# Loading q by pairs of tokens in the attention front of a RetNet and PReLU-MLP kernel, with a new instruction order

## The chip, the cores and the metric

The kernel runs on one core of a Trainium2 chip. The metric is device time in microseconds (us) of one execution; the times are medians of repeated runs.

## The reference

The attention is a retention layer without softmax; its output, seen as 4608 tokens of 512 features, goes through a two-layer MLP with a PReLU.

```python
# q, k, v: (8, 8, 576, 64) = batch, head, token, feature, float32
scores = matmul(q, k^T) / 8
gamma = 1 - 2 ** (-5 - head)
ret = scores * where(rel >= 0, gamma ** rel, 0)      # rel = row - column
attn = matmul(ret, v)
x = attn.transpose(0, 2, 1, 3).reshape(4608, 512)
h = x @ w_in                                          # w_in: 512 x 2048
g = maximum(h, 0) + alpha * minimum(h, 0)             # alpha: one per column of h
out = g @ w_out                                       # w_out: 2048 x 512
```

All inputs are float32; the two weights and alpha reach the kernel as 64-bit words, and it makes float32 of the weights itself.

## The kernel before

**Attention.** The 576 tokens of a head are nine chunks of 64. Within a chunk the scores are computed and masked; what earlier chunks contribute comes through a running state per head (64 x 64). The decay gamma is split into factors that depend on the token alone, so q, k and v only have to be scaled by tables (`tp`, made from `pf`, `dif` and `th` on DVE at the start).

**The front: parts.** The first two batches are done in six parts: parts 0, 1, 2 are chunks 0 to 3, 4 to 7 and 8 of batch 0, and parts 3, 4, 5 the same of batch 1. Parts 0, 1, 3 and 4 are the large ones. For a large part, `load_part` loads k, q and v as two tiles each (256 KB, 128 tokens in the partitions, eight heads of 64 features beside each other), so that the rows which the DMA moves have 64 floats (256 B). `part_scale` multiplies q and v by a table on POOL, in place. `part_transposes` turns k and q on PE, four 128x128 transposes for each tile, into a PSUM bank, and ACT copies them into SBUF. `part_scores` multiplies turned k and q by chunk on PE and masks on DVE into a room of its own (`at`). `part_states` and `part_values` make the states and the outputs, which ACT copies into x. `last_part` does the small parts. All later batches go pair by pair of heads through `joint`.

**The MLP.** Eight cells of the MLP run in the front with plain float32 matmuls (`unit_plain`, `second_plain`); `convert` makes their weights out of 64-bit words on ACT, DVE and POOL. The other cells use a split of x, g and the weights into pieces of lower precision (`split_roll`, `unit_roll`, `unit_two`, `second`), with matmuls of 128x128 by 512 columns.

**Dummy matmuls.** `fill` and `burn` put matmuls of a zero tile (`warm`) on PE at the start of the front; their results are not read.

**What sets the order.** Nothing is scheduled while the kernel is built. Each step is recorded by `do(engine, cost, function, reads, writes)` and gets a number; the list `ORDER` says in which order the steps are issued, which fixes the sequence on each engine, and the string `BANKS` says which PSUM bank each step gets. All loads and stores but one are issued by SP's queue. In the first `LIMITED` places of the order, a load also waits until at most `IN_FLIGHT` bytes (`IN_FRONT` in the first `FRONT` places) are under way:

```python
    LIMITED, IN_FLIGHT = 486, 5 << 18
    FRONT, IN_FRONT = 130, 4 << 18
```

POOL and DVE steps that are marked `lock=True` follow each other through a dependency in that order, across the two engines.

Of the kernel before, what the change touches and what calls it, by code (L numbers as in the profile page):

```python
# [10 lines left out]
FP32 = mybir.dt.float32  # L11
# [6 lines left out]
ALU = mybir.AluOpType  # L18
# [3 lines left out]
def kernel(  # L22
# [110 lines left out]
    for o, x, y in ((slice(0, 2), slice(0, 2), slice(3, 5)), (0, 0, 1), (0, 0, 2), (1, 0, 5)):  # L133
# [5 lines left out]
                                   in1=pf[:, 6], op0=ALU.mult, op1=ALU.mult)  # L139
    nc.vector.tensor_scalar(th[:, 2], dif[:, 6], 1.0, None, ALU.add)  # L140
# [8 lines left out]
    for i in range(2):  # L149
# [6 lines left out]
        "200535545661702405070423172047436234654317545707176141645461704500066171106600717116602607"  # L156
        "060167247052344635472107161067706117062653241061707601706104253461761006176107255234700761"
# [62 lines left out]
    RATE, RATE_256, RATE_128 = 265e3, 205e3, 115e3  # L220
# [17 lines left out]
    LIMITED, IN_FLIGHT = 486, 5 << 18  # L238
# [96 lines left out]

    def load_part(x, which=None):
        j0, j1 = PARTS[x % 3]
        for i, m in which or [(i, m) for i in range(3) for m in range((j1 - j0 + 1) // 2)]:
            s0 = (j0 + 2 * m) * C
            rows = min(P, j1 * C - s0)  # L340
            dma(lambda i=i, m=m, rows=rows: part(x, i)[0:rows, m],
                lambda i=i, s0=s0, rows=rows: (k, q, v)[i][x // 3, :, s0:s0 + rows].rearrange(
                    "h p d -> p h d"), rows * DM * 4, (), [key_p(x, i, m)], rate=RATE_256)

    def part_scale(x, i):
        j0, j1 = PARTS[x % 3]
        rows = min(P, (j1 - j0) * C)
        for m in range((j1 - j0 + 1) // 2):
            def f(m=m):
                t = part(x, i)[0:rows, m]  # L350
                return nc.gpsimd.tensor_tensor(
                    out=t, in0=t, in1=tp[0:rows, i - 1, m, :, None].to_broadcast([rows, H, D]),
                    op=ALU.mult)
            do("POOL", 1.05, f, (), [key_p(x, i, m)], lock=True)
# [8 lines left out]
    def part_transposes(x, i, bank):  # L363
# [6 lines left out]
        for m in range(2):  # L370
            pt = Gen(next(bank))

            def f(m=m, pt=pt):
                for c in range(NPAIR):
                    nc.tensor.transpose(pt.get()[:, c * P:(c + 1) * P],
                                        part(x, i)[:, m, 2 * c:2 * c + 2].rearrange(
                                            "p h d -> p (h d)"), ident)
            do("PE", 0.52 if x else 0.65, f, [key_p(x, i, m)], [(pt, 0)], size=8)

            def g(m=m, pt=pt):  # L380
                nc.scalar.copy(at()[:, :, m * P:(m + 1) * P],
# [3 lines left out]
    def part_scores(x, bank):  # L385
        a = Gen((gs[1], ats)[x // 3]) if x % 3 == 0 else room[x + 1, 2]

        def at():
            return words_of(a)[:, 0:1024].rearrange("p (h n) -> p h n", h=2)
        tat[x] = a, at  # L390
        (kt, kT), (qt, qT) = tT[x, 0], tT[x, 1]
        ps = [Gen(next(bank)) for _ in range(2)]
        for m in range(2):
            def f(m=m):
# [7 lines left out]
            do("PE", 0.58, f, [(kt, "t", m), (qt, "t", m)], [(ps[0], m), (ps[1], m)], kind="small",  # L402
               size=64)
        for h2 in range(2):
# [5 lines left out]
            do("DVE", 0.69, g, [(ps[h2], 0), (ps[h2], 1)], [(a, "m", h2)])  # L410
# [45 lines left out]
    def part_values(x, bank):  # L456
# [28 lines left out]
        for m in range(2):  # L485
# [16 lines left out]
            do("PE", 0.29 * len(js), g, [(qt, "t", m)] + [  # L502
# [1052 lines left out]
    for i, (va, vb) in enumerate(two):  # L1555
# [30 lines left out]
        "68-70 67 3 71 1-2 0 4-5 53 24 66 12 25 86 9 13-14 33 16 10 15 22 7 17 80 23 19 8 85 32 47 18 21 20 "  # L1586
        "27 48-50 84 6 115 83 51 26 64 55 52 28-29 56-57 87 81 118 58 119 88 30 59 62 82 63 40 114 116 65 60 "
        "154 112 34 31 54 117 110 113 11 72 111 36-37 139 61 136 138 140 38 142 35 153 141 137 171 41 43-44 "
        "89 39 42 168 143 94 166 144 95 103 73 145 90 45 146 46 155 147 181 156-157 209 182 75 170 183 76-77 "
        "102 158 74 159 91 93 160 92 212 161 184 162-163 204 78 121-122 97 176 185 129 96 98 177 99 104 100 "  # L1590
        "173 205 124 106 164 105 120 208 169 337 101 188-189 130 107-109 213 123 132 172 196 125-126 148 210 "
        "149 127 167 133 150 246 197 131 211 229 206-207 152 134-135 330 230 151 190 192-194 217 216 218 178 "
        "180 186 247 179 257 219 244 198 128 270 220 250 221 331 199 245 187 332 175 191 200 271 201-202 174 "
        "222 454 223 234-235 203 224-227 333 195 284-285 231 236 293 259 336 272 456 237 451 238-239 232-233 "
        "292 228 274 258 453 455 248 275 273 260-261 252 262 251 445 276 243 253 452 249 214 254 242 255 240 "
        "263 241 277 286 349 447 266 288 268 289-290 267 269 215 372 256 294 296-298 287 291 303 302 306 342 "
        "374 304 295 305 282 466 307 281 338 334 299 278 436 279 264 350 265 280 446 340 343 315 352-353 339 "
        "335 345 354 351 448 439 316 344 346 358 365 317 553 384 347 355 348 320 366 321 318-319 373 308 475 "
        "322 375 341 433 309 437 385 301 399 435 442 552 300 377 398 310-312 323-324 328 313 378 434 325 443 "
        "283 379 383 327 329 314 367 369 368 440 438 356 450 382 457 376 460 381 326 397 441 380 462 404 461 "  # L1600
        "79 415 414 360 467 413 361 405-410 402 458 411 400 412 417 419 359 362 416 363 423 422 421 165 364 "
        "403 401 444 392 463 393 386 459 387 468 357 465 481 555 482 420 424 449 388 418 394 426 464 396 425 "
        "472 490 370 473 395 522 488 519 523 483 520 526 489 495 529 487 507 469 496 389 497-498 390 499 524 "
        "501 505 427 506 478 504 517 500 503 539 493 485 568 371 502 428 492 484 521 530 527 476 528 534-535 "
        "540 532 541 516 508 533 430 391 542 491 536 543 537 544 494 545 470 538 582 486 514 474 480 581 509 "
        "583 477 510 512 511 513 515 431 471 618 595 584 531 588 570 590 596 546 597-599 569 586 563 548 585 "
        "594 547 593 571 549 564 607 587 479 601 604 600 561 589 616 562 565 620 572 566-567 573-575 606 554 "
        "592 634 603 619 605 636 602 577 591 432 635 617 614 551 608 576 615 610 550 637 578 621 638-639 "
        "622-623 640 651 609 612 655 624 652 429 648 641 653 611 613 658-661 654 662 674 579 643 665-668 656 "
        "697 647 669 663 670 695 671 696 664 688 672-673 690 675 689 580 677 687 657 649 642 644 698 645 650 "  # L1610
        "699-701 691-694 686 721 684 676 702 704 720 679 678 722 685 730 518 723 703 758 705 734-735 680-681 "
        "646 726 683 729 682 711 761 727 762 733 717 706 759 728 724 746 763 707-708 716 736 712 781 731 737 "
        "744 754 772 760 738-740 783 713-714 756 718 709 774-775 784 743 732 741 755 742 782 556 773 745 747 "
        "785-786 525 751 719 779 776 787 710 752-753 777 725 780 748 778 840 749-750 715 794-796 793 807 841 "
        "805 802 789 788 790 798 797 842 803 808-809 800 817 791 804 833 799 810 834 811-812 814 831 813 816 "
        "820 832 843 806 819 815 852 818 801 835 854 828-829 853 830 792 855-856 918 915 557 838 821 827 857 "
        "916 824 836 858 822 837 877 859 823 919 880 826 878 861 920 879 860 885 887 881 891 886 892-893 825 "
        "894 839 895 889 901 864 897 873 896 869 900 899 888 862 868 870-871 898 917 903 883 902 875 863 930 "
        "932 884 931 882 874 890 923 933 558-559 912 921 934 865-866 924 904 935 914 922 910 928 913 936 905 "
        "907 925 943 911 872 944 906 908 945-946 926-927 999 955 952 929 967 957 953 966 958-959 956 909 937 "  # L1620
        "954 876 948 960-962 939 942 969 949 951 991 1002 938 940 947 979 950 963 965 1004 968 998 1000 1003 "
        "1005-1007 992 964 867 757 971 989-990 993 1008 994 997 978 560 970 976 995 941 1028 625 1027 974 "
        "1029 1038 1001 977 1009 973 1010 975 1011 1050 1037 1041 1030 1068 1012 996 1065 1013 1042 1069 1014 "
        "1066 1015 1018 1067 1019 1051 1016 1071 1036 1035 972 1043-1044 1072 1020 1070 1073 1053 1034 1045 "
        "1047 1024 1046 1089 1033 1074-1075 1040 1049 1091 1048 1090 1063 1076 1052 1021 1079 1077 1092 1032 "
        "1055 1093 1039 1094 1060 1054 1064 1061 1095 1023 1017 1025-1026 1062 1031 1078 1059 1102 1056 1103 "
        "1111 1105 1104 1112 1141 1097 1110 1116 1106 1096 1098 1115 1099 1107 1100 1058 1113 1125 1148 1139 "
        "1057 1127 1117-1120 1122 1109 1121 1142 1114 1140 1126 1154 1150 1128 1152 1108 1153 1155 1143-1145 "
# [179 lines left out]
```

## Time and profile before

| | |
|---|---|
| median of 3 runs | 915.4 us (915.34 to 915.81) |
| the profiled execution's own time | 915.47 us |
| its span, first to last instruction | 913.4 us |
| PE busy | 906.3 us (99%) |
| DVE, ACT, POOL busy | 549.6, 500.7, 520.3 us |
| DMA share, 0 to 30 us and 30 to 112 us | 0.99 and 0.92 |
| DMA share, 112 to 913 us | 0.47 |

The profile is one execution. Busy times are of instructions, and an engine's idle time matters only where the engine that ends last waits for it. Times below that begin with a start are microseconds from the span's start. PE is TensorE's matmuls, PEld its weight loads, DVE VectorE, ACT ScalarE, POOL GpSimd, SP the engine whose queue issues the DMAs.

### The profile page before, as it was taken

What the parts mean: (1) busy time and instruction counts of PE and PEld (TensorE: products, weight loads), DVE (VectorE), ACT (ScalarE), POOL (GpSimd) and SP (SyncE); (2) the same over time, 40 slices, a digit from 0 to 9 for tenths busy, and PEclk for the clock granted to TensorE, in tenths of its full rate; (3) what the DMA queues carried; (4) which work ended last, traced back from release to release, by engine and by line L of the source; (5) the groups of instructions that cost most, each with busy time, mean ns of one, the idle gap of its engine ahead of it and who ended that gap; (6) DMA issues with size and microseconds to landing.
All of it is one profiled execution on the core that took longest, in us unless ns stands there. A gap on an engine that the chain in (4) does not pass through costs nothing. (4 is left out here: it accounts for less than half of the span.)

```text
span 913.4 us, 19163 instructions
## 1 busy us (share of the span) xinstructions
PE 906.3 (99%) x7331; PEld 739.6 (81%) x7331; DVE 549.6 (60%) x1004; ACT 500.7 (55%) x1011; POOL 520.3 (57%) x461
## 2 busy tenths in 40 slices
PE   9999999999999999999999999999999999999998
PEld 8767788887788888888888888888888888888886
DVE  5797767757768776576756776434444534444243
ACT  4575665556555665666746565636363636364441
POOL 4587665556556665756542335666655657574624
PEclk9999999999999999999999999999999999999999
DMA  9999778788898888775243332212122222211112
GB/s 204 245 232 185 172 173 184 166 204 186 185 200 192 205 208 189 177 182 167 70 141 130 99 115 82 70 58 81 57 93 64 91 82 76 93 47 47 46 47 70
DMA packets 235948, 121.34 MB, mean 133 GB/s; under 512 B 203456, under 2 KB 203728, under 8 KB 235856
## 3 DMA queue, kind: packets, MB, share of 16 engines
q1 hardware_dynamic: 235712, 119.98, 52.3%
q8 instruction: 58, 0.95, 0.5%
q14 instruction: 34, 0.28, 0.1%
q10 hardware_dynamic: 144, 0.13, 0.0%
HBM read 74.19 MB, written 32.51 MB: 117 GB/s over the span
## 5 line engine op out<-in xcount | busy, mean ns | idle before, releaser
L1223 PE MATMUL pso<-w,g 128*128 128x512 f32 x1344 | 330.3, 392 | 0.0
L1223 PEld LDWEIGHTS pso<-w,g 128*128 128x128 f32 x1344 | 249.9, 188 | 54.3 <-POOL g L1150 1.6
L1147 POOL TENSOR_TENSOR g<-ga_all,g 128x512 fp32r<-128x512 f32 x76 | 98.2, 1295 | 131.5 <-ACT g L1143 101.8
L1150 POOL TENSOR_TENSOR g<-g 128x512 fp32r<-128x512 f32 x114 | 147.3, 1295 | 19.4 <-DVE su L949 5.7
L1071 PE MATMUL psa<-lx_x,w 128*128 128x512 f32 (+1 forms) x288 | 70.3, 377 | 0.2 <-DVE at L824 0.2
L1071 PE MATMUL psh<-lx_x,w 128*128 128x512 f32 (+1 forms) x272 | 68.2, 384 | 0.1
L1143 ACT ACTIVATE g<-ga_all 128x512 fp32r<-128x512 f32 x76 | 47.8, 631 | 36.6 <-PE pso L1223 17.5
L1139 POOL TENSOR_TENSOR g<-g 128x512 fp32r<-128x512 f32 x22 | 28.5, 1297 | 61.8 <-DVE g L1136 34.4
L1071 PEld LDWEIGHTS psa<-lx_x,w 128*128 128x128 f32 x288 | 51.4, 188 | 12.1 <-issue 1.3
L1071 PEld LDWEIGHTS psh<-lx_x,w 128*128 128x128 f32 x272 | 49.6, 188 | 11.2 <-issue 0.6
L1223 PE MATMUL pso<-lx_x,g 128*128 128x512 f32 x216 | 53.5, 390 | 0.1
L1147 POOL TENSOR_TENSOR g<-vn,g 128x512 fp32r<-128x512 f32 x25 | 32.4, 1297 | 37.2 <-ACT g L1143 34.5
L1145 ACT ACTIVATE g<-ga_all 128x512 fp32r<-128x512 f32 x76 | 47.2, 624 | 5.8 <-PE pso L1223 4.0
L1046 POOL TENSOR_TENSOR lx_x<-lx_x 128x512 fp32r<-128x512 f32 x28 | 35.9, 1293 | 23.1 <-DVE lx_x L1043 18.9
L1223 PEld LDWEIGHTS pso<-lx_x,g 128*128 128x128 f32 x216 | 40.4, 188 | 9.0 <-DVE o L1246 0.6
L1241 DVE TENSOR_TENSOR op<-pso,op 128x512 f32<-128x512 f32 x35 | 24.0, 686 | 31.2 <-PE pso L1223 31.2
L1071 PE MATMUL pso<-lx_x,w 128*128 128x512 f32 (+1 forms) x160 | 37.8, 370 | 0.0
L1105 PE MATMUL psh<-w,w 128*128 128x512 f32 x144 | 34.6, 389 | 0.0
L1105 PE MATMUL psa<-w,w 128*128 128x512 f32 x144 | 34.6, 389 | 0.0
L716 POOL TENSOR_TENSOR qx<-qx,tabx 128x576 f32<-128x576 f32 x24 | 27.6, 1149 | 9.6 <-DMA qx<-in_q_dram 5.9
L1071 PEld LDWEIGHTS pso<-lx_x,w 128*128 128x128 f32 x160 | 28.0, 188 | 5.7 <-ACT o L1245 0.6
L1147 POOL TENSOR_TENSOR g<-x,g 128x512 fp32r<-128x512 f32 x13 | 16.9, 1298 | 26.2 <-ACT g L1143 24.7
(408 smaller groups left out, 1968.2 us busy)
## 6 DMA issues: line engine op xcount, KB each, us to landing
xk<-x SPq DMA_DIRECT2D x18, 512.0 KB, 3.7
ok<-o SPq DMA_DIRECT2D x36, 256.0 KB, 2.7
op<-ok SPq DMA_DIRECT2D x18, 512.0 KB, 4.0
out_dram<-o SPq DMA_DIRECT2D x35, 256.0 KB, 2.3
x<-xk SPq DMA_DIRECT2D x16, 512.0 KB, 5.5
kx<-in_k_dram SPq DMA_DIRECT2D x96, 72.0 KB, 3.3
qx<-in_q_dram SPq DMA_DIRECT2D x96, 72.0 KB, 3.3
kn<-in_k_dram SPq DMA_DIRECT2D x48, 144.0 KB, 3.6
```

The lines of the kernel that those rows point to most:

```text
L716: return nc.gpsimd.tensor_tensor(out=qh, in0=qh, in1=tabx[:, None, c, :, None].to_broadcast([P, NJ, 2, 32]), op=ALU.mult)
L1046: do("POOL", 1.29, lambda h=h, l=l, d=d: nc.gpsimd.tensor_tensor(out=piece(d()), in0=h(), in1=l(), op=ALU.subtract), [(g, 0, n), (g, 1, n) ...
L1071: nc.tensor.matmul(out_of(p), w[:, c0:c0 + P], xp(l, cc), start=(l != 1 and cc == 0), stop=(l > 0 and cc == NCC - 1))
L1105: nc.tensor.matmul(p.get(), w[:, c0:c0 + P], piece(words_of(g)[:, o:o + DM]), start=(l != 1 and cc == 0), stop=(l > 0 and cc == NCC - 1))
L1139: do("POOL", 1.29, lambda: nc.gpsimd.tensor_tensor(out=piece(to.get()[:, 2]), in0=to.get()[:, 0], in1=to.get()[:, 1], op=ALU.subtract), [( ...
L1143: do("ACT", 0.64, lambda: nc.scalar.mul(piece(to.get()[:, 2]), whole(), BELOW), both, [(to, 2)])
L1145: do("ACT", 0.64, lambda: nc.scalar.mul(piece(to.get()[:, 0]), whole(), BELOW * 2.0 ** -12), both, [(to, 0)])
L1147: do("POOL", 1.29, lambda: nc.gpsimd.tensor_tensor(out=piece(to.get()[:, 1]), in0=whole(), in1=to.get()[:, 2], op=ALU.subtract), both + [( ...
L1150: do("POOL", 1.29, lambda: nc.gpsimd.tensor_tensor(out=piece(to.get()[:, 2]), in0=to.get()[:, 0], in1=to.get()[:, 1], op=ALU.subtract), [( ...
L1223: nc.tensor.matmul(a[2 * m + b].get(), piece(g.get()[:, l, f, m * P:(m + 1) * P]), w_piece(u, 2 + f, l), start=(cell["first"] and f == 0 a ...
L1241: do("DVE", 0.69, lambda: nc.vector.tensor_tensor(out=t(), in0=p1.get(), in1=t(), op=ALU.subtract), [(p1, 0)], [tk])
```

## The change

q of the four large parts is loaded so that a partition holds two neighbouring tokens of a head: 128 floats (512 B) in a row, for four heads at a time, and each such 256 KB is loaded by two DMAs of 128 KB, one for the even heads and one for the odd. POOL scales q by a new table `tq` (two columns for each head, one for each of the two tokens), no longer in place: it writes into the room that takes the masked scores later, with the heads in the order in which they are transposed. The transposes read that room; ACT's copy of their result puts the two tokens of a pair back beside each other (every second word). A transposed half now holds all 256 tokens of four heads, instead of 128 tokens of eight, so that scores and values name both halves. `ORDER` and `BANKS` are new for the first part of the program, and `LIMITED` goes from 486 to 500.

```diff
+    tq = const.tile([P, 2, 2 * NPAIR], FP32, name="tq")
+    tq_of = [tq.rearrange("p h (c e) -> p h c e", e=2)[:, :, :, e] for e in range(2)]
+    def by_pairs(t):
+        return t.rearrange("p (c h) -> p h c", h=2)
+    nc.vector.scalar_tensor_tensor(out=tq_of[0], in0=by_pairs(tp[:, 0, 0]), scalar=1.0 / QSCALE,
+                                   in1=by_pairs(tp[:, 0, 0]), op0=ALU.mult, op1=ALU.mult)
+    nc.vector.scalar_tensor_tensor(out=tq_of[1], in0=by_pairs(dif[:, 0]), scalar=1.0,
+                                   in1=tq_of[0], op0=ALU.add, op1=ALU.mult)
...
-    LIMITED, IN_FLIGHT = 486, 5 << 18
+    LIMITED, IN_FLIGHT = 500, 5 << 18
...
+    def twos(x, i):
+        return i == 1 and x % 3 < 2
+    def part_q(x, m):
+        return spot_p(x, 1)[:, m * DM:(m + 1) * DM]
+    def turned_q(x, m):
+        return tat[x][1]().rearrange("p h n -> p (h n)")[:, m * DM:(m + 1) * DM]
     def load_part(x, which=None):
...
+            if twos(x, i):
+                for h2 in range(2):
+                    dma(lambda m=m, h2=h2: part_q(x, m).rearrange(
+                            "p (h c f) -> p h c f", h=2, f=P)[:, h2],
+                        lambda m=m, h2=h2: q[
+                            x // 3, 4 * m + h2:4 * m + 4:2, j0 * C:j1 * C].rearrange(
+                                "c (p e) d -> p c (e d)", e=2), P * DM * 2, (),
+                        [key_p(x, i, m) + (h2,)], rate=RATE_512)
+                continue
...
     def part_scale(x, i):
...
+        if twos(x, i):
+            a = Gen((gs[1], ats)[x // 3]) if x % 3 == 0 else room[x + 1, 2]
...
+                    return nc.gpsimd.tensor_tensor(
+                        out=turned_q(x, m).rearrange("p (n h d) -> p h n d", h=2, d=D),
+                        in0=part_q(x, m).rearrange("p (h n d) -> p h n d", h=2, d=D),
+                        in1=tq[:, :, 4 * m:4 * m + 4, None].to_broadcast([P, 2, 4, D]), op=ALU.mult)
+                do("POOL", 1.05, f, [key_p(x, i, m) + (h2,) for h2 in range(2)], [(a, "r", m)], lock=True)
+            return
...
     def part_transposes(x, i, bank):
...
-            do("PE", 0.52 if x else 0.65, f, [key_p(x, i, m)], [(pt, 0)], size=8)
+            do("PE", 0.52 if x else 0.65, f,
+               [(tat[x][0], "r", m) if twos(x, i) else key_p(x, i, m)], [(pt, 0)], size=8)
...
+                if twos(x, i):
+                    nc.scalar.copy(
+                        at()[:, 2 * m:2 * m + 2].rearrange("p c (t e) -> p c e t", e=2),
+                        pt.get().rearrange("p (c e t) -> p c e t", c=2, e=2))
+                    return
...
     def part_scores(x, bank):
...
-            do("PE", 0.58, f, [(kt, "t", m), (qt, "t", m)], [(ps[0], m), (ps[1], m)], kind="small",
-               size=64)
+            do("PE", 0.58, f, [(kt, "t", m), (qt, "t", 0), (qt, "t", 1)], [(ps[0], m), (ps[1], m)],
+               kind="small", size=64)
...
-            do("DVE", 0.69, g, [(ps[h2], 0), (ps[h2], 1)], [(a, "m", h2)])
+            do("DVE", 0.69, g, [(ps[h2], 0), (ps[h2], 1)], [(a, "m", h2), (a, "r", h2)])
...
-            do("PE", 0.29 * len(js), g, [(qt, "t", m)] + [
+            do("PE", 0.29 * len(js), g, [(qt, "t", 0), (qt, "t", 1)] + [
```

What the new `ORDER` does, as the built program shows it: SP's first loads were k, q, q, k, v, v of part 0 (256 KB each) and are now q, q (128 KB each), v, q, q, k, k, v. A q load of part 3 now stands ahead of the small part's k, and the k of part 4 stands later. On PE the steps up to the 112th are in another order, from the 113th on in the same one; on the other engines the steps after that stretch stand in the same order too. SP issues eight loads more, DVE runs two instructions more, PE, ACT and POOL have as many as before.

## The prediction

> **What bounds the kernel now.** I read the busy shares first, then PE's waits, then PE's and SP's timelines of the first 30 us, because the built programs differ only there (below).
>
> ```profile
> span 913.4 us, 19163 instructions
> ...
> PE 906.3 (99%) x7331; PEld 739.6 (81%) x7331; DVE 549.6 (60%) x1004; ACT 500.7 (55%) x1011; POOL 520.3 (57%) x461
> ...
> q8 instruction: 58, 0.95, 0.5%
> ```
>
> PE has something to do in all but 7 us. The last line is the instruction fetches: 58 packets of 16 KB on the same DMA engines; 0.5% of 16 x 913.4 us over 58 is about 1.26 us each.
>
> ```profile
> PE psh L1297 <- DVE warm L101: 1.1, 1, 1.1
> PE psa L535 <- DMA w<-in_k_dram: 0.4, 1, 0.4
> PE pso L422 <- POOL w L351: 0.4, 1, 0.4
> PE psa L470 <- ACT ga_all L980: 0.3, 1, 0.3
> PE psa L375 <- DMA w<-in_k_dram: 0.2, 1, 0.2
> ```
>
> PE's waits by length: all but the first are in the attention's front and end on loads of k and v or on their scaling. On PE's timeline:
>
> ```profile
> 19.98 0.63 PE L375 MATMUL psa<-ident,w 128*128 128x128 f32 x4 [0.25 <-DMA w<-in_k_dram]
> ...
> 22.95 0.27 PE L422 MATMUL pso<-w,w 64*64 64x64 f32 x2 [0.36 <-POOL w L351]
> ...
> 28.48 0.71 PE L535 MATMUL psa<-ident,w 64*128 64x64 f32 x8 [0.37 <-DMA w<-in_k_dram]
> ```
>
> From a step's start to the next one's, against the quarter mark of all equal steps, these three cost 0.41, 0.57 and 0.64 us, and one at 73.65 costs 0.37: 2.0 us in all. That is nearly everything a better front can win. The rest is fixed: 30 dummy matmuls of L1288 and 96 of L1297 stay, and the first four groups of transposes run 0.85 us apart against 0.44 later, a half-speed PE until about 11 us (the page's clock row does not show it), whatever the load order.
>
> ```profile
> 4.11 0.87 SPq L224 DMA_DIRECT2D w<-in_v_dram  x1
> 5.30 0.86 SPq L224 DMA_DIRECT2D w<-in_v_dram  x1
> 6.50 0.84 SPq L224 DMA_DIRECT2D lx_w<-in_moe_w_in_dram  x1
> 7.71 0.34 SPq L224 DMA_DIRECT2D lx_w<-in_moe_w_in_dram  x1
> ```
>
> SP issues one load per landing here (1 MB may be in flight), so the spacing is the price of a load: 1.20 us for 256 KB in rows of 256 B. DMA share is 0.99 over 0 to 30 us: the stream of loads sets PE's front.
>
> **The change, part by part.** PE has the same 5364 matmuls in both programs. On every engine the order is the same, step for step, from PE's 113th step on (111.6 us in the trace); before that it is shuffled. So 80% of the span is carried over and moves as a block.
>
> Faster loads. Eight loads of q (256 KB each; parts 0, 1, 3, 4) become 16 of 128 KB with rows of 512 B. No row of the trace has 512 B. Rows of 256 B cost 1.20 x 16 / 1024 = 18.8 ns; two loads with 2048 B rows land 0.66 us apart (12.28, 12.95), so 82.5 ns each. On a straight line between, a 512 B row costs 27.9 ns, a load 512 x 27.9 / 16 = 0.89 us, a saving of 0.31 us. Ends: it costs as two of 256 B (saves nothing), or as one (saves 0.60). I take 0.31, as 512 B is nearest to the 256 B row and the line has its fixed part from it.
>
> The Trainium skill (DMA: Bandwidth & Descriptors, Specifications) puts the least size for line rate at 512 B, with a read-modify-write below it; by that rule a load would move at the 2048 B rows' rate and save 0.54 us. No run here shows a 512 B row yet; it is the faster rival's case.
>
> Costs hidden. Eight more issues on SP (0.36 to 0.9 us each): SP waits for landings anyway. Two DVE instructions for `tq`, 0.2 us each behind `tp` (ready at 4.5 us): the first q scaling can start at 5.0, and PE burns dummies until 6.4; without that cover they cost 0.4 us. The q scaling on POOL (L351, 1.04 us) writes another tile with a swapped middle order: between 1.04 and the 1.30 of a POOL multiply or subtract with two full operands (L1147); I take 1.04, as one operand is still a broadcast table; at 1.30 the first point below comes 0.26 us later. The ACT copy now writes every second word: between 0.59 (L381) and 0.67 (L615, which reads and writes every second word); I take 0.63, four hundredths more, hidden behind PE's other groups. The masked-scores room is taken earlier, but its last readers are 10 us or more behind in each case.
>
> The new wait. Each transposed q half now holds four heads instead of two chunks, so every scores and values step needs both halves. Queued behind a late half are, on PE, all scores, states and plain matmuls.
>
> First point, scores of part 1. The second piece of q's first half comes after the same set of loads that before ended with the second half of k (landed 18.71): 18.71 - 4 x 0.31 = 17.5. POOL 1.04 gives 18.55, PE's transposes 18.6. PE arrives at 12.67 + 1.44 + 0.52 + 0.58 + 0.98 + 0.44 + 0.41 + 0.58 + 0.45 = 18.07 (to-next times of the same steps before): a new stall of 0.5 us. With 2.6 us of transposes and dummies behind it, the scores start at 21.2 (21.43 before). The stalls of 0.41 and 0.57 shrink to this 0.5: v lands 1.24 earlier, its scaling ends at 21.6, and the states start at 22.16. The two plain groups end at 26.75.
>
> Second point, part 2's transposes (28.48 before, released by its k, landed 28.44). In the new SP order a 256 KB q load of part 3, which landed at 29.53, stands ahead of that k. So k lands at 29.53 - 5 x 0.31 = 28.0, and PE waits 1.25 us for it: what was won goes into one stall. Gain 0.46 us.
>
> Third point, from 28.0 to k's transposes of part 4. Their k load now stands behind 18 loads that before came partly later. The load of v for part 3 lands at 45.96 + 1.15 (one k load and half a q load more, a 72 KB load less) - 6 x 0.31 = 45.25; then 12.4 us of loads by size (0.66, 1.2, 1.3 us a piece) and three fetches of about 0.8 us: 60.05. PE arrives at 28.02 + 34.25 (28.48 to 62.73 before) - 2.80 (three steps moved behind) + 0.44 (one ahead) = 59.9. A loss of 0.2 us, with 1 us of doubt. The states of part 3, moved from 53.3 to 46.3, have 0.4 us to spare.
>
> Sum: -0.46 + 0.2, about -0.3 us. The profiled execution took 915.47 us (span 913.4 and 2.1 around it), 0.07 above the median of 915.4: so 915.1.
>
> **Rivals.** A measurement of this kernel can tell about 0.2% (1.8 us) from no change.
>
> Faster: rows of 512 B move at the long rows' rate (0.54 saved). Part 2's k lands at 29.53 - 2.7 = 26.83, the first point has no stall (PE would arrive at 26.1), part 4's k is early: -1.6 us, and -2.0 if the stall at 73.65 goes too: 913.5. For it: the line's fixed part is a guess from one size. Against: it needs every other wait in the shuffled 80 us to stay away.
>
> Slower: the order overdraws the load stream. If 512 B rows save under 0.05 us a load, part 2's k lands at 29.53 and PE starts there 1.1 us later than before; part 4's k comes at 62.4 against PE at 61.45, 0.95 more: +2.0 us, 917.4. The same comes from one instruction fetch more ahead of each k (1.26 us), where the packets of a load wait on one engine. For it: both k loads are now the last to land, with no slack. Against: the line says 0.31.
>
> No effect at all on the front (fetches fall so that the losses move but add up as before): 915.4, inside the forecast's case.
>
> **How the numbers follow.** Forecast (savings of 0.1 to 0.45 a load; -1.5 to +1.5): 0.47, its own range 913.9 to 916.9. Faster rival 0.24: every stall must go, and 2.0 us is all there is. Slower rival 0.29: nothing caps what a late load costs, and half a dozen steps of the new order have under 0.5 us to spare. The range for 8 in 10 takes most of both: 913.3 to 917.8.
>
> **What would show it.** In the profile of the changed kernel: SP's issues at the start closer together after q loads (0.4 to 0.45 us a piece); a PE wait at the first L375 twin of part 1 near 18 us and a longer one at part 2's transposes (released by `w<-in_k_dram`) near 28.0; part 4's k transposes near 60 us; PE's first `lx_x` matmul, 102.25 before, about 0.3 us earlier. The sum is wrong if part 2's transposes start before 27 us, or if a wait of over 1 us shows between 30 and 111 us.

## The result: slower by 0.22%

Medians of 17 executions of each kernel on one chip: 915.39 us before (914.39 to 916.13) and 917.25 us after (916.17 to 919.91). The ratio is 1.0022, with a 95% interval of 1.0014 to 1.0029. Forecast were 915.1 us and no measurable change. The profiled execution of the changed kernel took 916.17 us, the shortest of its 17: its trace shows 0.7 of the 1.86 us that the medians differ by. Part of the rest goes with the clock: in 5 of the 17 the mean granted clock was 0.998 or less, and those have a median of 918.74 us, against 916.84 us for the other 12.

The page's header and busy shares after:

```profile
span 914.4 us, 19177 instructions
...
PE 906.5 (99%) x7331; PEld 740.0 (81%) x7331; DVE 550.3 (60%) x1006; ACT 502.5 (55%) x1011; POOL 519.7 (57%) x461
```

PE works as long as before (906.5 against 906.3 us); the longer span is idle time. PE's waits after (us in total, times, longest):

```profile
PE pso L416 <- POOL w L383: 1.3, 1, 1.3
PE psh L1341 <- DVE warm L101: 1.1, 1, 1.1
PE psa L466 <- issue: 1.0, 1, 1.0
PE psa L1115 <- DVE at L868: 0.2, 1, 0.2
```

L416 is `part_transposes` and L466 `part_states` (L375 and L422 before); L383 is the new scaling of q. The waits on k are gone. In their place stand one long wait on q's scaling and a stall that ends on "issue": the profile shows no engine and no load that PE waited for. In PE's timeline from 18 us to 112 us only two rows have a wait:

```profile
19.73 0.66 PE L416 MATMUL pso<-ident,w 128*128 128x128 f32 x4 [1.31 <-POOL w L383]
...
24.78 0.27 PE L466 MATMUL psa<-w,w 64*64 64x64 f32 x2 [0.95 <-issue]
```

The windows (length; busy time and instructions of PE, PEld, DVE, ACT, POOL; clock; DMA share; GB/s) show what this costs; before first:

```profile
18.00:30.00 12.00, 10.87 (x236) 9.12 (x238) 8.03 (x14) 6.80 (x12) 7.63 (x8) 1.00 1.09 232
62.00:80.00 18.00, 17.70 (x248) 11.36 (x246) 15.39 (x26) 12.08 (x23) 14.48 (x14) 1.00 1.06 206
```

and after:

```profile
18.00:30.00 12.00, 9.74 (x177) 8.30 (x176) 7.71 (x14) 7.48 (x13) 9.83 (x10) 1.00 0.91 234
62.00:80.00 18.00, 18.00 (x288) 11.84 (x288) 14.79 (x27) 13.40 (x25) 15.67 (x15) 1.00 1.03 224
```

From 18 to 30 us PE is busy 1.13 us less than before, from 62 to 80 us 0.30 us more; over the first 112 us it is 108.47 against 109.24, 0.77 less. The 113th step, from which the order is the old one, starts at 112.43 us against 111.58, and the rest is carried to the end.

**Why q came late.** On SP's queue after (start, length):

```profile
0.81 0.94 SPq L233 DMA_DIRECT2D w<-in_q_dram  x2
...
2.31 1.09 SPq L233 DMA_DIRECT2D w<-in_q_dram  x2
...
7.85 2.43 SPq L233 DMA_DIRECT2D lx_w<-in_moe_w_in_dram  x2
10.32 0.96 SPq L233 DMA_DIRECT2D w<-in_q_dram  x2
```

SP spends about 0.5 us on each 128 KB piece, which takes 0.45 us to move (256 rows at 27.9 ns over 16 engines), so at the start it can't keep the transfers fed. At 7.85 it then spent 1.95 us on issuing one weight load, while an instruction fetch was on its way (7.83 to 9.14). The windows of before and after over those stretches:

```profile
2.00:4.00 2.00, 2.00 (x42) 2.00 (x42) 1.69 (x11) 0.09 (x1) 0.90 (x6) 1.00 1.03 229
10.00:11.00 1.00, 1.00 (x33) 0.87 (x36) 0.00 (x0) 0.59 (x1) 0.85 (x2) 1.00 1.00 314
```

```profile
2.00:4.00 2.00, 2.00 (x42) 2.00 (x42) 1.69 (x11) 0.09 (x1) 0.91 (x6) 1.00 0.75 201
10.00:11.00 1.00, 1.00 (x47) 0.70 (x49) 0.00 (x0) 0.76 (x2) 0.05 (x1) 1.00 0.51 158
```

The DMA share falls to 0.75 and 0.51 in stretches that were full before. The last piece of q of part 1 was issued at 13.53 us and landed at 18.57. How much of its delay is SP's pace and how much the new place of the load among the others, no run separates: the first run in the old order below has an even longer issue (2.30 us at 6.18), and there PE doesn't wait for q. POOL's timeline shows what that makes late:

```profile
17.39 1.04 POOL L383 TENSOR_TENSOR w<-w,tq 128x512 f32<-128x512 f32 x1 [5.39 <-DMA w<-in_q_dram]
18.64 1.04 POOL L383 TENSOR_TENSOR w<-w,tq 128x512 f32<-128x512 f32 x1 [0.21 <-DMA w<-in_q_dram]
```

The two engines take the halves of this q in opposite order: POOL scales the second half first, and PE's first transposes are those of the first half. So PE waits for the half that is scaled last; it ends at 19.68 and PE goes on at 19.73. The other half was ready at 18.43, when PE fell idle, but its transposes (0.4 to 0.5 us) stand behind. In the old order both engines take the second half first, and the new order has them agree in the other three large parts. With the two transposes exchanged PE could have done one in its idle time, an estimate of up to 0.5 us that no run tests.

**The stall on "issue".** PE stops inside the states of part 1, at its 962nd instruction (matmuls, weight loads and PE's semaphore instructions counted in order of start; where a weight load is the 962nd, its matmul is the next). The DMA view from 22.0 to 22.9 us has one instruction packet:

```profile
q8 instruction: 1, 0.02, 7.1%
```

It runs from 22.32 to 23.35 us, and there is none from 18 to 22 us; PE resumes at 24.78. Before, PE has no such stall.

### The profile page after: what moved, and what is told of

Same layout as the page of the kernel before. It is cut to its first block, busy times and chain, and to the rows that moved or that the text cites. A ratio compares the mean times of both kernels' runs of the same rounds, so it can differ in the third digit from the quotient of the medians.

```text
span 914.4 us, 19177 instructions
## 1 busy us (share of the span) xinstructions
PE 906.5 (99%) x7331; PEld 740.0 (81%) x7331; DVE 550.3 (60%) x1006; ACT 502.5 (55%) x1011; POOL 519.7 (57%) x461
## 5 line engine op out<-in xcount | busy, mean ns | idle before, releaser
L1187 ACT ACTIVATE g<-ga_all 128x512 fp32r<-128x512 f32 x76 | 47.8, 631 | 36.9 <-PE pso L1267 17.5
L868 DVE SCALAR_TENSOR_TENSOR at<-psa,pf,mask 64x64 f32<-64x64 f32 (+1 forms) x48 | 24.6, 516 | 13.5 <-PE psa L847 4.6
```

Source lines behind the costliest of these rows:

```text
L868: nc.vector.scalar_tensor_tensor(out=mt.get()[half(1 - h2), h2, j], in0=fro[x], scalar=pf[x, 1, h:h + 1], in1=mask[x, None, :].to_broadcas ...
L1187: do("ACT", 0.64, lambda: nc.scalar.mul(piece(to.get()[:, 2]), whole(), BELOW), both, [(to, 2)])
```

## Experiments

Two things are in question: what the faster loads are worth, and what the new order costs. Each ratio is to the kernel before on the same chip, with its 95% interval. Kernels called "in the old order" have the change's loads, scaling and copies with before's `ORDER` and `BANKS`. The "113th step" is the first common one.

**The changed kernel once more**, as a base for the next three.

> The changed kernel once more, for a second profiled execution. In the first one PE has two stalls that the kernel before lacks: 1.3 us at the transposes of q of part 1 (19.73 us, released by POOL) and 1.0 us in the middle of the first states step of part 1 (24.78 us, put down to issue). Theory A (both belong to the order: the last piece of q lands late, and a block of PE's instructions is fetched late): both come again, with lengths that differ by up to 1 us, since loads and fetches share the DMA engines, and the time is 916 to 918. Theory B (the stalls are chance of one execution): they are gone in this profile, and the time of it is below 916.

Measured: 918.60 us, 1.0025 (1.0014 to 1.0037). In this execution the loss sits elsewhere: nothing waits at q's transposes; the stall at the 962nd instruction is 1.6 us (packet 22.51 to 23.39, PE back at 25.08) and waits on k take 0.8. The 113th step starts at 113.32, 1.74 later than before, and the time is 1.59 longer. The last piece of q landed at 18.22, 0.35 earlier, and PE came to it 0.9 us later (19.4 us for 18.4), after a wait of 0.4 us on k at 9.6 and with the full clock from 12.3 us in place of 10.3. So the q wait depends on how late PE already is; the stall comes back.

**Is it the instruction block?** Sixteen tiny matmuls ahead of q's transposes move every later instruction by 64 places:

```diff
+            for x in range(tiny):
+                a = half(x % 2)
+                nc.tensor.matmul(unread.get()[a, 0:16], warm[a, 0:C], warm[a, 0:16], start=True, stop=True)
-    for _ in range(3):
-        fill(2, 0.25)
+    for tiny in (16, 0, 0):
+        fill(2, 0.25, tiny=tiny)
```

> 16 tiny dummy matmuls (64 of PE's instructions, some 0.9 us) are added ahead of q's transposes of part 1, in PE's idle time of 1.3 us. Theory A (the 1.0 us stall is PE waiting for a 16 KB block of its own instructions): the next block is asked for some 64 instructions, so 2 to 3 us, earlier; the stall inside the states step vanishes, or, if the fetch is not earlier, it moves 64 instructions forward into the scores. The states end up to 1.0 us earlier; k of part 2, landed at 28.76, then holds PE, so 0.6 us are won at 28.8 us and 0.4 to 0.6 in the end: 916.7 where the changed kernel has 917.2. Theory B (the stall belongs to the states step itself, a wait that the trace does not name): it stays 1.0 us in the same instruction and the time stays 917.2. The added dummies cost nothing in either (at most 0.1 us if they outlast the wait).

Measured: 918.68 us, 1.0032 (1.0021 to 1.0042). The packet comes at 18.68, and the 962nd instruction no longer waits. A stall shows at the 1474th instead, exactly 512 later (packet 32.40 to 33.36). PE's timeline, and from its waits the row of another stall:

```profile
34.69 0.27 PE L537 MATMUL pso<-w,w 64*64 64x64 f32 x2 [1.98 <-issue]
...
PE pso L1049 <- issue: 1.4, 1, 1.4
```

The other stands at 82.14 us, at the 2754th instruction (packet 79.32 to 80.57), 1280 behind the 1474th: the places are whole multiples of 256 apart. It is among matmuls of 128x512 that follow each other every 0.43 us, so short matmuls are not a condition. So the stall is tied to PE's place in its instruction stream, not to data. It wasn't removed but moved, and the two together are 3.4 us, where the one before was 1.0 to 1.6.

**Old order, new loads.**

```diff
+    (ORDER and BANKS of before)
-    LIMITED, IN_FLIGHT = 500, 5 << 18
-    FRONT, IN_FRONT = 130, 4 << 18
+    LIMITED, IN_FLIGHT = 494, 5 << 18
+    FRONT, IN_FRONT = 136, 4 << 18
```

> The change without its new order: the new loads, scaling, transposes and copies of q, in the order (and PSUM banks) of the kernel before, the two pieces of a half of q issued one after the other. Theory A (the new order's two stalls are the loss): no stall over 0.6 us in the first 30 us, 914.5 to 915.6, so the kernel before or up to 0.9 us better by the shorter loads. Theory C (the new wait, scores behind both halves of q, costs wherever it stands): part 1's scores start 0.5 to 1.5 us later than before's 21.43, and the time is 916.3 or more.

Measured: 914.96 us, 0.9986 (0.9977 to 0.9994): faster than before. PE's timeline from 18 to 112 us has a single wait, and no stall on "issue":

```profile
28.29 0.70 PE L579 MATMUL psa<-ident,w 64*128 64x64 f32 x8 [0.96 <-DMA w<-in_k_dram]
```

The same kernel again:

> The change in the old order once more, on the chip of the two mixed orders, with a second profile. Every theory: no wait of PE over 0.2 us before 20 us, full clock between 10.5 and 12 us, no stall put down to issue over 0.3 us; part 2's k holds PE 0.8 to 1.3 us at 28.3 us; ratio 0.998 to 0.9995.

Measured: 914.80 us, 0.9995 (0.9986 to 1.0003); wait on k 0.7 us, 113th step at 110.98. The two together put the loads in the old order at 0.05 to 0.14% less than before, at the edge of what can be told. The changed kernel is 0.27 to 0.39% longer than these, so its order costs 2.5 to 3.6 us.

**Rows of 256 B again**, in the new order and in the old one; these load other tokens of q.

```diff
-    q[x // 3, 4 * m + h2:4 * m + 4:2, j0 * C:j1 * C].rearrange("c (p e) d -> p c (e d)", e=2)
+    q[x // 3, 4 * h2:4 * h2 + 4, (j0 + 2 * m) * C:(j0 + 2 * m + 2) * C].rearrange("h p d -> p h d")
```

> The changed kernel with the 16 pieces of q loaded in rows of 256 B (other tokens of q than the reference's arrangement; sizes, order and all other work are the same). Rows of 512 B took 27 to 28 ns in the changed kernel's trace, rows of 256 B 18 ns, so a pair of pieces should cost 0.3 us more. Theory A (the rows are priced right, the load stream sets PE's front): the last piece of part 1's q lands 4 x 0.3 = 1.2 us later, near 19.8, the stall there grows from 1.3 to about 2.5 us, k of part 4 lands 1.6 to 2 us later: 918.5 to 919. Theory D (512 B rows bring nothing, since the stream waits for issues and landings): 917.2 as the changed kernel.

> The change in the old order, with the 16 pieces of q loaded in rows of 256 B (other tokens of q; sizes, order and all other work the same). The old order with rows of 512 B was 1.2 us faster than the kernel before (ratio 0.9986). Theory A (that gain is the shorter rows): it goes, 0.9996 to 1.001. Theory D (the gain is something else, such as the smaller pieces or the scaling that frees k, q and v's tiles): it stays, 0.998 to 0.999.

Measured: 920.20 us, 1.0044 (1.0031 to 1.0057) in the new order, 1.6 us over the changed kernel on the same chip; 916.51 us, 1.0007 (0.9997 to 1.0016) in the old one, with a wait of 1.7 us on part 2's k (transposes at 29.34). The gain of the old-order kernel goes with the long rows: its first run (0.9986) lies clear of 1.0007, the second (0.9995) less so, and in the new order the intervals of the pair meet. The first of the two also shows a further cost, in its windows:

```profile
23.00:26.50 3.50, 1.88 (x104) 1.68 (x94) 2.26 (x4) 1.33 (x3) 2.72 (x3) 1.00 1.02 257
26.50:29.90 3.40, 3.40 (x9) 2.69 (x10) 3.37 (x8) 0.67 (x1) 0.83 (x1) 0.50 1.00 218
30.00:33.00 3.00, 3.00 (x25) 2.27 (x27) 0.76 (x3) 1.17 (x2) 1.35 (x2) 1.00 0.80 200
```

After a stretch in which PE idled 1.6 us the granted clock is 0.50 for 3.4 us, and a plain group of 1.83 us takes 3.45.

**Four tiny matmuls only** (`(4, 0, 0)`, 16 instructions), which move the block's end off the states without reaching the next place.

> The changed kernel with 4 tiny dummy matmuls (16 of PE's instructions) ahead of q's transposes of part 1, where 16 of them took PE past the place that asks for the next block of instructions and moved a later block's edge into a burst of small matmuls, with a new stall of 2.2 us. Theory A (the stalls sit at fixed counts of PE's instructions, 256 apart: the 962nd, the 1474th): with 16 more instructions the fetch comes before the wait, near 18.7 us, the 1.0 to 1.6 us stall at the 962nd is gone, and the 1474th now falls among large matmuls, where the block has time; k of part 2 then holds PE until about 28.8: 0.6 to 1.2 us less than the changed kernel (ratio to the kernel before 1.001 to 1.0018, where it had 1.0022 and 1.0025). Theory B (16 instructions are not enough to ask earlier): the stall stays, 1 to 1.6 us at the 962nd instruction, ratio as the changed kernel's.

Measured: 917.22 us, 1.0017 (1.0007 to 1.0027). The packet comes at 20.56, and neither the 962nd nor the 1474th instruction stalls. But other waits replace most of it: 0.6 us at the early transposes (9.67; the clock is full only from 15.0 us, against 10.3), 0.3 on part 2's k and some 0.5 us at 75 us, in waits that end on DVE. The 113th step is at 112.79, in the changed kernel's profiles at 112.43 and 113.32. Without the stall the ratio is 0.05 to 0.08% lower, some 0.5 to 0.7 us, which is inside the intervals.

**Other loads first** (with the four tiny matmuls), so that k comes earlier at the start:

```diff
-        "4 3 68 6 2 1 73 5 0 72 70 69 7 15 ...
+        "5 4 68 3 0 2 73 1 6 72 70 69 7 15 ...
```

> As the run with 4 tiny matmuls, and the first eight loads in another order: k's first half first, k's second half ahead of the second half of q, v last. Theory A (in the new order k of part 0 comes last of six loads, and when a fetch of instructions falls before it, PE waits 0.8 to 1.0 us at 8 to 10 us): that wait is gone in every profile, and the time is 0.2 to 0.8 us below that of the run with 4 tiny matmuls alone (0 where its profile shows no such wait). Theory C (v, now last, holds PE at the first states step near 10.3 us instead): an equal time, with a wait on POOL's scaling of v.

Measured: 917.49 us, 1.0017 (1.0006 to 1.0027). The wait on k at the start turns into one of 1.2 us on q's scaling (7.7 to 8.9), which neither forecast had; part 2's transposes start at 28.46. Nothing is gained in all.

**Part 2's k ahead**, in the old order: its k and q issued before two weight loads of 512 KB.

```diff
-        "... 42 118 120 ... 158 ...
+        "... 158 157 74 118 120 ...   (and steps 42 to 48 exchanged with 74 to 80)
```

> The change in the old order, with k and q of part 2 loaded ahead of two 512 KB loads of expert weights, and these two (with their conversions on ACT, DVE and POOL) exchanged. In the old order with the change PE's one wait beside the start is 1.0 us (1.3 us without an instruction started) for k of part 2 at 28.3 us. Theory A (that wait is all that is left there, and the steps behind it have room): transposes of part 2 near 27.2, 0.7 to 1.1 us less in the end, ratio to the kernel before 0.9974 to 0.998. Theory E (the next load or weight conversion takes its place): a wait of 0.5 to 1 us between 30 and 65 us, ratio 0.998 to 0.999.

Measured: 916.38 us, 1.0002 (0.9994 to 1.0011). The transposes start at 27.41, 0.88 earlier than in the first old-order run, and all of it is lost again at once, as the weights and a scaling are now late:

```profile
PE pso L1049 <- ACT w L659: 0.8, 1, 0.8
PE psa L416 <- POOL at L383: 0.5, 1, 0.5
```

**Which part of the order?** First, the changed kernel (with four tiny matmuls) with part 0's steps as in the old order; then the old order with part 0's steps as in the new one:

```diff
-        "4 3 68 6 2 1 73 5 0 72 70 69 7 15 ...        new order
+        "5 1 68 2-4 73 0 6 72 70 69 7 14 ...          new order, old start
-        "70-72 69 5 73 1-4 0 6-7 55 26 68 14 ...      old order
+        "70-72 69 4 73 3 6 2 1 5 0 7 55 26 68 15 ...  old order, new start
```

> As the run with 4 tiny matmuls in the new order, with the steps of part 0 (its eight loads, four transposes, scores and states) put back into the old order. In five of the six runs of the new order PE waited 0.4 to 1.2 us for k or q of part 0 between 7.5 and 10.3 us, and the full clock came at 9.7, 12.3, 12.9, 13.5 and 15.0 us; in the four of the old order no wait there is over 0.15 us and it came at 10.9 to 11.4. Theory A (the waits delay the grant of the full clock by one step of 3.41 us, worth up to 1.7 us): no wait over 0.2 us before 12 us, full clock by 11.5, the first fill group of six dummies at 12.9 or before (14.9 in the run with 4 tiny matmuls), and 0.4 to 1.2 us less in the end (k of part 2 near 28.8 takes the rest): ratio to the kernel before 1.0004 to 1.0013, where it had 1.0017. Theory F (the start is paid for anyway at k of part 2): full clock early, but k of part 2 holds PE at 29.0 or later, ratio 1.0014 to 1.002.

> The change in the old order, but with the steps of part 0 (its loads, transposes, scores and states) in the new order's sequence: the mirror of the run before. Theory A: a wait of 0.4 to 1.2 us between 7.5 and 10.3 us, full clock at 12 to 15 us, q's transposes of part 1 begin 0.5 to 2 us later than in the old order; k of part 2, which held PE 1.0 us there, takes up to 1.3 us of it, so the ratio is 0.999 to 1.0005 (0.9986 with the old start), and in profiles with the late clock the wait for that k is gone. Theory F (the start does not matter): ratio 0.998 to 0.999.

Measured: 917.03 us, 1.0014 (1.0005 to 1.0022), and 916.66 us, 1.0007 (0.9998 to 1.0016). In the first, PE runs 1.25 us ahead of the changed kernel until 46.5 us, and from 48 us only 0.21: it has met the next loads of the new order. At 75 us it loses 0.6 us more, in waits that end on DVE, and from there it is 0.5 us behind.

```profile
PE psh L466 <- POOL w L392: 0.8, 1, 0.8
PE pso L579 <- DMA w<-in_k_dram: 0.7, 1, 0.7
```

The first of these is at part 3's states, whose v landed at 46.84, as in the changed kernel (46.95). In the second, waits of 0.3 and 0.7 us at 7.5 and 9.7 us appear and the full clock comes at 15.0 us instead of 10.9; part 2's transposes start at 29.73 (28.29). So the new start alone costs 1.9 us in the old order (1.1 us against the second old-order run, where the intervals meet), while mending it in the new order gains almost nothing.

**Fewer dummies ahead**, old order: 96 PE instructions less before part 0.

```diff
-        burn(8)
+        fill(2, 0.43) if i in (0, 1, 4, 5) else burn(8)
```

> The change in the old order, with four of the six groups of 8 tiny dummy matmuls at the start replaced by 2 wide ones each (128 x 128), which take as long (0.85 us) but are 96 fewer of PE's instructions. Theory A (PE fetches its instructions in blocks of 256 and stands when it reaches the 1218th or the 1986th before the block is there): the asking for the block of the 1218th falls behind the wait for k of part 2, 28.3 us, and PE reaches that instruction some 1.8 us later in the middle of small matmuls: a stall of 1 to 1.7 us at the 1218th instruction near 31 us that the old order does not have, perhaps one of 0.5 to 1.2 us at the 1986th near 57 us; ratio 0.9995 to 1.001 where the old order has 0.9986. Theory B (these stalls are not tied to the count of instructions): no stall put down to issue over 0.6 us, ratio 0.998 to 0.999. Wide dummies may also bring the full clock up to 3.4 us earlier than 10.9 us; k of part 2 hides what that wins.

Measured: 916.11 us, 0.9999 (0.9988 to 1.0011). The clock is full from 7.2 us, earlier than in any other kernel, but the stall is back at the 962nd instruction (0.5 us; packet 22.65 to 23.73, PE back at 25.01), and not at the 1218th, where I had put it. At the 1986th, the other place I had named, it is 0.2 us (1986 is four times 256 beyond 962):

```profile
PE psa L579 <- DMA w<-in_k_dram: 0.5, 1, 0.5
PE psh L466 <- issue: 0.5, 1, 0.5
```

**Where in the front does the new order lose?** Old order up to part 2's transposes and new behind; new up to 31.5 us and old behind.

> The changed kernel with all instructions that the old order has ahead of part 2's transposes (28.3 us of PE) in the old order, and everything behind them in the new order. Theory A (all of the new order's loss is made before part 2's transposes): as the old order with the change, ratio to the kernel before 0.998 to 0.9995. Theory G (part of it is made later, at v of part 3, 47 us, and k of part 4, 61 us, whose loads the new order takes early or late): a wait of 0.3 to 1 us at one of the two in the profile, ratio 1.0005 to 1.002.

> The mirror: the new order up to the second transposes step of part 2 (31.5 us of PE), the old order behind it. Theory A: as the changed kernel, ratio 1.0012 to 1.0025, with the stall at PE's 962nd instruction, 1 to 1.6 us, or a wait at part 0 and a late clock. Theory G: 0.9986 to 1.0005, since the old order behind it has room to take 1 us back.

Measured: 918.70 us, 1.0033 (1.0020 to 1.0046), and 919.53 us, 1.0047 (1.0034 to 1.0060). Both halves come out worse than either whole, because the seams have waits of their own: two of 1.4 us in the first, after which the clock is half for 6.8 us, and one of 2.0 us on k in the second. They don't answer the question. The second has the new order's front and no stall at the 962nd instruction: its packet came at 18.21 us, where the changed kernel's came at 22.32 and 22.51. What delays the packet stays open.

**Two loads of parts 3 and 4 earlier**, on the new order with the old start:

```diff
-        "... 217 254 ... 179 ... 205 338 ... 250 ...
+        "... 217 179 254 ... 205 250 338 ...
```

> As the run of the new order with the old start and 4 tiny matmuls, where PE came to part 3's states 1.25 us earlier than in the changed kernel and gave all of it back: 1.0 us there, waiting for POOL's scaling of v (its load landed at 46.84, in the changed kernel at 46.95), and the rest before k of part 4 (landed 61.20; 61.07). Two loads are moved up: the second half of v of part 3 by one place, ahead of a piece of q, and the second half of k of part 4 by five places, ahead of four small loads for the rest blocks and one of q. Theory G (the new order's later loads set a floor for PE, whatever happens in the first 30 us): the wait at part 3's states shrinks from 1.0 to 0.5 us or less, k of part 4 lands before 59 us, its transposes begin at 60.4 to 60.9 (61.3 to 61.5 in the changed kernel and in the run with the old start), 0.5 to 1.0 us less in the end: ratio to the kernel before 1.0003 to 1.0010 (1.0014 without the two moves). Theory H (another wait takes its place, as at every step mended so far): ratio 1.0012 to 1.002.

Measured: 918.93 us, 1.0031 (1.0018 to 1.0044). The wait at part 3's states goes, but PE had lost 1.3 us at q's scaling and 1.8 us on part 2's k before either moved load was issued, so it says nothing on what the two are worth.

**More bytes in flight at the start**, old order: 1.25 MB and 1.5 MB instead of 1 MB.

```diff
-    FRONT, IN_FRONT = 136, 4 << 18
+    FRONT, IN_FRONT = 136, 5 << 18        (6 << 18 in the second)
```

> The change in the old order, with 1.25 MB of loads allowed in flight in the first 136 places of the order in place of 1 MB. In the old order with 1 MB the DMA share was 0.79 and 0.83 over 0 to 18 us in two profiles (0.92 before the change), and k of part 2 held PE at 28.3 and 28.0 us, only 0.2 to 0.4 us earlier than before, although four loads of q stand ahead of it that each take 0.3 us less. Theory J (the shorter loads leave holes, since SP may issue only when one of the few loads in flight has landed, and a load that waits for one ring holds the rest up): DMA share 0.85 to 0.95 over 0 to 18 us, part 2's transposes at 27.0 to 27.7, 0.3 to 0.8 us less: ratio to the kernel before 0.998 to 0.999 (0.9986 and 0.9995 with 1 MB). Theory K (more in flight makes the urgent loads and the fetches of instructions wait longer): k or v of part 0 hold PE at 9 to 12 us, or a stall put down to issue of over 0.5 us; ratio 0.9995 to 1.001.

> As the run with 1.25 MB, with 1.5 MB in flight. Theory J: as with 1.25 MB or up to 0.3 us better. Theory K: longer waits than with 1.25 MB, ratio 1.000 to 1.0015.

Measured: 914.54 us, 0.9985 (0.9976 to 0.9994), and 914.58 us, 0.9990 (0.9978 to 1.0001). With 1.25 MB part 2's transposes wait for nothing:

```profile
27.33 0.71 PE L579 MATMUL psa<-ident,w 64*128 64x64 f32 x8
...
18.00:30.00 12.00, 11.57 (x294) 10.17 (x296) 8.41 (x15) 7.47 (x15) 7.62 (x8) 1.00 1.02 263
```

From 18 to 30 us the loads move 263 GB/s, against 231 and 235 with 1 MB, and the 113th step starts at 110.28 (111.27 and 110.98). In times the gain over the old-order kernel is inside the intervals; against before, this is the best version, 0.15% faster. 1.5 MB brings nothing more.

## Why the prediction was wrong

By its own sum the change should have won 0.3 us; it lost 1.86 us, clear of the noise. What held: the tail from the 113th step on (88% of the span, not 80%) is carried over as a block (0.85 late there, 0.70 in the time; 1.74 and 1.59 in the second profile). The row price held: packets of 512 B take 27 ns in the median (33 in the mean), where 27.9 was forecast; those of 256 B take 18 (20.6 to 21.7 in the mean) and those of 2048 B 84. By the means a load of 256 KB saves 0.26 to 0.33 us, where 0.31 was forecast. By 18 us the stream had moved 266 KB more (214 against 199 GB/s), close to four times 0.31 us at 212 GB/s; that it fits so well is in part luck, since the loads of that stretch are not the same ones and the DMA share fell from 0.92 to 0.87. (The statement that no row of the trace before has 512 B was wrong: one small load of alpha has them, at 27 ns.) By the least size for line rate that the Trainium skill gives (DMA: Bandwidth & Descriptors, Specifications) a 512 B row would by estimate take a quarter of 84, 21 ns; the trace disagrees. POOL's 1.04 us held exactly, and ACT's copy took 0.63 us as forecast.

What failed, by its steps:

1. **"Eight more issues on SP: SP waits for landings anyway."** False in the first microseconds and in the long issue at 7.85, where SP is what sets the pace. The last q piece landed at 18.57 for 17.5. That, and the order of the two halves, makes the stall of the first point 1.3 us where 0.5 was forecast, with the scores at 22.44 for 21.2.
2. **A term was missing: PE's own instruction blocks.** I had priced fetches as DMA time alone (0.8 us each; the packets of the first 112 us took 0.9 to 1.9 us). The new order puts the end of a block into the states of part 1, and PE stands for 1.0 to 1.6 us there, in both profiles of the changed kernel and in that with 256 B rows, though not in the one with the old order behind. This is the largest recurring error: the tiny-matmul runs moved and removed it, and the old order never showed it at that place until 96 instructions were taken out ahead.
3. **Second point.** Part 2's k landed at 28.76 for 28.0, but PE was later still (29.39 for 26.75) and didn't wait for it: a loss of 0.91 us against before, where a gain of 0.46 was in the sum. Of the 2.6 us by which PE was late, 1.2 come from the first point and 1.2 from the stall, in which PE started nothing from 23.61 to 24.78.
4. **Third point.** Part 4's k landed at 61.07 for 60.05, at the end of the doubt of 1 us given to it. The error came before it: part 3's v, from which that time was reckoned, landed at 46.95 for 45.25. In the first profile PE came to this k no earlier and didn't wait; in the second it waited 0.4 us.
5. **"A half-speed PE until about 11 us, whatever the load order."** Full clock came anywhere between 7.2 and 15.0 us in these kernels. The same wait of 0.6 us near 10 us came with 15.0 us in one kernel and with 9.7 in another; counted in steps of 3.41 us from the full clock, it lay within one step in the first and mostly behind the end of a step in the second, so its place may decide, which no run tests.

The forecast's sum of -0.3 us was made of savings that are real but of a size with three costs left out. The slower rival named a time near the result, 917.4 us, by a mechanism that did not act: its rows were to save nothing, and they saved about what was forecast; that it came so near is luck. The faster rival fell at its rate.

What the runs settle and what they don't: the long rows gain, the order loses more than that; the start of the order alone loses 1.1 to 1.9 us in the old order; in the new one the traces show PE standing at the block's end, and the times can't tell what that is worth. Mending any one of these in the new order brought at most 0.7 us, none of it clear of the intervals, since the next wait takes its place. How the 2.5 to 3.6 us of the new order split among its places stays open; the three runs meant for that did not tell.

## What to carry to other kernels

Test a change of data movement apart from a new instruction order: here the one gains and the other loses, and only the old order with the new loads shows it. Price an order by the slack at each wait, and count among the waits those that no data explains: PE's instruction blocks, the time that the issuing queue takes at the start, and the idle time that puts off the full clock. Check that two engines take the halves of one tile in the same order. One profile is one execution: two of the same kernel lost at different places.

## What the runs showed of the hardware

- **Instruction blocks.** Stalls on "issue" of 0.5 to 2.0 us stand at PE's 962nd, 1474th and 2754th instruction (and one of 0.2 at the 1986th), whole multiples of 256 apart. Each of the longer ones is behind a 16 KB packet of 0.9 to 1.3 us; PE resumes 1.3 to 1.7 us after the packet's end. The profile of the changed kernel has 58 such packets for PE's 14847 instructions, one less than 58 times 256, and that with 96 fewer has 57. The Trainium skill (Runtime: NRT & Kernel Launch, Instruction fetch mechanics) gives 16 KB blocks of 256 instructions, which agrees with these places, and calls the cost of a block's end mostly hidden; at most of these places the traces show no stall, at those named they do.
- **The clock in steps.** In all 19 profiles the granted clock, once full, stays so for a whole multiple of 3.413 us (such as 901.12 and 904.53), and the two stretches at half clock in the midst last 3.41 and 6.83 us. The Trainium skill (TensorE: Matmul & The Clock Gate, Part 1) has a free-running window of that length; the traces agree. Counted in these steps, 1.62 us of PE's idle time within one (the run with 256 B rows) and 1.86 (old order up to part 2's transposes) were followed by half clock, while 1.60 (the changed kernel's second profile), 1.69 (new order up to 31.5 us) and 1.77 (two loads earlier) were not. So neither the length of the idle time nor its lying within one step decides alone; what does stays open. With the six groups of tiny matmuls at the start the full clock came at 9.7 to 15.0 us, with wide ones in place of four of them at 7.2 (one profile).
- **SP's issue beside a fetch.** One DMA issue took 1.95 us at 7.85 in the changed kernel, 1.81 at 13.68 and 2.36 at 25.39 in the kernel before, each while an instruction packet was under way; the usual ones take 0.3 to 0.9 us. Of the issues of the first 112 us in all 19 profiles, 145 of the 383 that meet such a packet take over 1.2 us, and 56 of the 1947 that meet none (the changed kernel has one of 1.77 at 42.05). So the packet makes a long issue likely but is not its only cause.
